# Two attention layers and two FFNs at one new token: keeping four key tiles and two value tiles on the chip between the passes

## The chip, the cores and the metric

The kernel runs on one core of a Trainium2 chip. The core has a matrix engine (PE, with its weight loads PEld), a vector engine (DVE), a scalar engine (ACT), GpSimd (POOL), and a sync engine (SP) that issues nearly all transfers; 16 DMA engines move data from HBM to SBUF. SBUF and PSUM have 128 partitions; PSUM has 8 banks of 2 KB in each partition. The metric is the device time of one launch in microseconds (us), as a median over runs.

## The reference

`B=2` rows of one token go through attention, FFN, attention, FFN, with the same weights and the same caches in both rounds:

```python
x = x + _A_ref(_layernorm(x), k_cache, v_cache, wq, wo)   # H=16, Sk=4096, Dh=256, D=448
x = x + _B_ref(_layernorm(x), W_gate, W_up, W_down)       # F=1792
x = x + _A_ref(_layernorm(x), k_cache, v_cache, wq, wo)
x = x + _B_ref(_layernorm(x), W_gate, W_up, W_down)

# _A_ref
q = (x @ wq).reshape(B, Sq, H, Dh).transpose(0, 2, 1, 3)
scores = jnp.einsum("bhqd,bhkd->bhqk", q, k_cache) * (Dh ** -0.5)
o = jnp.einsum("bhqk,bhkd->bhqd", softmax(scores), v_cache)
return o.transpose(0, 2, 1, 3).reshape(B, Sq, H * Dh) @ wo

# _B_ref
gate, up = x @ W_gate, x @ W_up
return (gate * (gate > 0) * up) @ W_down
```

All of it is float32. A head of one row has keys of 4096 x 256 and values of the same size, 4 MB each.

## The kernel before

**Units and passes.** A unit is one head of one batch row: 32 of them. Pass 1 (`first`) takes them in order 0 to 31; pass 2 (`second`) takes the last four backwards and then 0 to 27, so that what pass 1 left on the chip can be used at once. Between the passes stands the turn: the first FFN (`ffn(False)`), and after pass 2 the last FFN (`ffn(True)`). The unit that is number 12 of pass 1 (`first[12]`) is number 16 of pass 2, and `first[11]` is number 15.

**The arena.** SBUF holds one large tile, `arena`, of 27 slots of 2048 columns (1 MB each): three blocks of 8 slots, and three single slots. A block takes a pair: the values of one unit and the keys of the next one, 16384 columns or 8 MB, by one transfer (L131). Single slots take a head's projection weights (`w_head`) or a part of the FFN's weights, which are 1792 columns wide each. A transfer is issued as soon as its slots have been released (`pump`), in one fixed list for both passes, all on SP's queue. A block comes free when the keys have been reduced (`score_block`) and the values have been weighed (`weigh`). Some chunks (`keep`) stay from the end of pass 1 to the start of pass 2.

**A unit's work.** Keys lie with 32 rows of 256 in each partition; a key tile is one such row over the 128 partitions, 128 KB. In the steady part, DVE multiplies all 32 tiles by the query in place (L378, 8192 columns) and reduces them to 32 scores per partition (L386). Then come the maximum over the partitions on POOL (L429), the exponential on ACT (L434 and L437) and its sum on POOL (L443). One unit later PE multiplies the probabilities with the values (`weigh`, L462, 16 matmuls of 512 columns: two value tiles each), ACT and DVE add the two halves of the result into `row` (L475 `out_copy`, L478 `out_add`), and PE turns it into a column (L488). With every second unit PE also projects the head (L511), computes the next head's queries (L338), and ACT and POOL spread them over the partitions (L350, L354).

**Order around the change.** Each engine runs its instructions in the order in which the loop at L527 writes them: for unit `u` the scores of `u`, the end of `u-2`, the softmax of `u`, then the weighing of `u-1` and its `out_copy`.

**PSUM before.** `ps_o` has one tile `po` over two banks for the attention's output, even units in the first and odd ones in the second. `ps_f` has two rotating banks `pf` for the first queries of a pass and for the FFN's products. `ps_q`, `ps_s` and `ps_a` take the other four.

Of the kernel before, what the change touches and what calls it, by code (L numbers as in the profile page):

```python
# [27 lines left out]
ALONE = 25  # L28

# [41 lines left out]
def two_layers(  # L71
# [18 lines left out]
    ps_f = ctx.enter_context(tc.tile_pool(name="ps_f", bufs=2, space=PSUM))  # L90
# [5 lines left out]

    units = Arena()
    pending = []
    at_of = {}
    blocks = set()  # L100

    def source(key, n):
        kind, name, c = key
        if kind in "kv":
            h, b = name
            at = (h * B + b + (kind == "v")) % (H * B)
            c += NC * (kind == "k" and n < PAIR)
            return vk[at, :, c * UNIT : (c + n) * UNIT]
# [6 lines left out]
    def pump():  # L115
        while pending:
# [7 lines left out]
            dst = arena[:, at * UNIT : at * UNIT + src.shape[1]]  # L124
# [14 lines left out]

    def get(*key):  # L140
        at = at_of[key]
        return arena[:, at * UNIT : (at + 1) * UNIT]
# [90 lines left out]
    po_all = ps_o.tile([P, 2, 2 * DH], F32, name="po")  # L233
    nc.vector.memset(po_all, 0.0)
# [60 lines left out]
    def attention(order, after, q_first=None, begun=None):  # L295
# [60 lines left out]
        def first_query():  # L356


            if q_first is None:
                total = squares()  # L360
                query_of(0, ps_f.tile([P, B, DH], F32, name="pf"))
            else:
                q_of[0] = q_first
                total = begun()
            deviation(total)
            query_of(1, ps_f.tile([P, B, DH], F32, name="pf"))
# [3 lines left out]
        def score_block(u, c):  # L370
# [4 lines left out]
            if c == 0:  # L375
                s_of[u] = work.tile([P, NT], F32, name="scores")
            if c == 0:
                nc.vector.tensor_mul(kt, kt, q_of[u][:, None, :].to_broadcast([P, NT, DH]))  # L378
# [6 lines left out]
            if c == NC - 1:  # L385
                nc.vector.reduce_sum(s_of[u][:, shared:], kt[:, shared:, :], axis=AX.X)  # L386
# [65 lines left out]
        def weigh(u, c):  # L452
# [5 lines left out]
            if c == 0:  # L458
                po_of[u] = po_all[:, u % 2]
            for t in range(CT // 2):  # L460
# [4 lines left out]
                    vt[:, 2 * t * DH : (2 * t + 2) * DH],  # L465
# [94 lines left out]
    def ffn(last):  # L560
# [9 lines left out]
        def proj(parts):  # L570

            p = ps_f.tile([P, D], F32, name="pf")
# [42 lines left out]
        pg = proj([(0, 0, True), (1, 1, True), (2, 2, True), (3, 3, False)])  # L615
# [18 lines left out]
        pu = proj([(3, 4, True), (4, 0, True), (5, 1, True), (6, 2, True)])  # L634
# [8 lines left out]
        ph = ps_f.tile([P, FULL, P], F32, name="pf")  # L643
# [31 lines left out]
        if last:  # L675
# [9 lines left out]
            y_end = ps_f.tile([P, TAIL], F32, name="pf")[SUMS : SUMS + B]  # L685
            nc.tensor.matmul(y_end, unit, y_end_row, start=True, stop=False)
            pds = [po_all[:, 0, :D], ps_f.tile([P, D], F32, name="pf")] * 2
# [28 lines left out]
        q = ps_f.tile([P, DH], F32, name="pf")  # L716
# [13 lines left out]
        pd = po_all[:, 0, :D]  # L730
# [104 lines left out]
```

## Time and profile before

| | us |
|---|---|
| median of 3 runs | 1320.66 (1320.5 to 1320.78) |
| the profiled execution | 1320.27 |
| its span, first to last instruction | 1318.5 |
| DVE busy | 1081.6 |
| PE busy | 553.7 |
| POOL busy | 269.0 |
| ACT busy | 195.6 |
| moved from HBM | 562.56 MB |

The page of the profile gives, from top to bottom, busy time by engine, the span in 40 equal slices, the DMA queues, and a chain that ends with the last instruction: at each step it goes back to what released that step. A piece of the chain that is named DMA runs from the issue of a transfer to its landing, so it holds the time in which the transfer stood behind others in the queue. In groups and timelines, a bracket at the end of a row is the idle time of the engine just before the instruction, and what ended it.

### The profile page before, as it was taken

Reading aid. Unit: us, or ns where it says so; the run is one execution under the profiler, and the core shown is the slowest. Engines: PE = TensorE matmul, PEld = TensorE weight load, DVE = VectorE, ACT = ScalarE, POOL = GpSimd, SP = SyncE. Lnnn points to the kernel's source line nnn. Section 1 sums busy time; section 2 is a strip of 40 time slices with the busy share of each in tenths; the row PEclk is TensorE's granted clock in tenths of the full one; section 3 lists DMA queues with packets and bytes.
Section 4 is the critical chain, followed back from the end, with each engine's and each line's share of the span. In section 5 each row is a group of like instructions: output and inputs, shape, how many; then the busy total and the mean of one; then the engine's idle time right before and its main releaser. Section 6 shows DMA issues by size and latency. Waiting matters only on the chain.

```text
span 1318.5 us, 9085 instructions
## 1 busy us (share of the span) xinstructions
PE 553.7 (42%) x3276; PEld 190.6 (14%) x3276; DVE 1081.6 (82%) x780; ACT 195.6 (15%) x776; POOL 269.0 (20%) x192
## 2 busy tenths in 40 slices
PE   2243342433434324345585444242433424434348
PEld 2011010110111101112141111110111101101113
DVE  4989888898888988888729987798888988877892
ACT  2100000000000000212026513000000000012241
POOL 0002003322133220321001153030123331230210
PEclk9675666656667667666697777666767667666679
DMA  9999999999999999999999999999999999999998
GB/s 408 435 430 429 432 428 437 432 436 434 417 445 435 430 430 426 445 418 430 421 405 416 431 430 435 438 432 430 432 431 436 433 428 436 429 432 425 427 425 334
DMA packets 22665, 563.16 MB, mean 427 GB/s; under 512 B 2520, under 2 KB 2652, under 8 KB 9564
## 3 DMA queue, kind: packets, MB, share of 16 engines
q1 hardware_dynamic: 22612, 562.57, 99.5%
q8 instruction: 26, 0.43, 0.1%
q14 instruction: 19, 0.16, 0.0%
q10 hardware_dynamic: 8, 0.00, 0.0%
HBM read 562.56 MB, written 0.00 MB: 427 GB/s over the span
## 4 chain that ended last, share of the span: by engine, by line
DMA 55%; DVE 32%; PE 7%; POOL 2%; issue 2%; ACT 1%; DVEq 0%; SPq 0%; POOLq 0%; ACTq 0%
DMA arena<-in_vk_dram 54%; DVE arena L378 12%; DVE scores L386 11%; DVE arena L409 3%; DVE down L418 2%; PE po L462 2%; POOL top L429 2%; DVE arena L418 2%; DMA arena<-in_w_out_dram 1%; DVE row L478 1%; PE small L488 1%; PE acc L511 1%; DVE scores L415 1%; ACT arena L411 1%; PE pf L576 1%
## 5 line engine op out<-in xcount | busy, mean ns | idle before, releaser
L378 DVE TENSOR_TENSOR arena<-arena 128x8192 f32<-128x8192 f32 x51 | 443.3, 8692 | 111.0 <-DMA arena<-in_vk_dram 110.9
L386 DVE TENSOR_REDUCE scores<-arena 128x32 f32<-128x8192 f32 (+1 forms) x53 | 431.8, 8148 | 0.0
L488 PE MATMUL small<-ones,row 128*128 128x1 f32 x256 | 62.0, 346 | 686.3 <-DVE row L478 686.3
L462 PE MATMUL po<-arena,probs 128*2 128x512 f32 x2048 | 303.1, 734 | 10.3 <-DMA arena<-in_vk_dram 6.6
L429 POOL PARTITION_ALL_REDUCE top<-mx x64 | 64.6, 1009 | 645.8 <-DVE mx L427 645.8
L443 POOL PARTITION_ALL_REDUCE total<-rs x64 | 176.1, 2752 | 61.3 <-ACT probs L437 60.3
L488 PEld LDWEIGHTS small<-ones,row 128*128 128x128 f32 x256 | 56.5, 308 | 748.9 <-DVE row L478 748.9
L434 ACT ACTIVATE nm<-top,nsr 128x1 f32<-128x1 f32 x64 | 18.8, 294 | 612.4 <-POOL top L429 612.4
L354 POOL PARTITION_BROADCAST arena<-arena x58 | 27.6, 545 | 300.6 <-ACT arena L350 300.6
L462 PEld LDWEIGHTS po<-arena,probs 128*2 128x2 f32 x2048 | 54.8, 96 | 198.3 <-issue 191.2
L338 PE MATMUL pq<-arena,xs 128*33 128x256 f32 x174 | 70.6, 571 | 14.1 <-DMA arena<-in_w_head_dram 14.1
L511 PE MATMUL acc<-arena,oT 128*2 128x448 f32 x128 | 50.9, 894 | 32.1 <-DVE oT L501 32.1
L350 ACT ACTIVATE arena<-pq 33x256 f32<-33x256 f32 x29 | 10.9, 377 | 321.7 <-PE pq L342 321.7
L382 ACT ACTIVATE arena<-arena 128x256 f32<-128x256 f32 x104 | 41.7, 402 | 86.2 <-DVE arena L378 86.2
L478 DVE SCALAR_TENSOR_TENSOR row<-po,lead,row 128x256 f32<-128x256 f32 x64 | 30.7, 479 | 25.8 <-ACT row L475 25.4
L411 ACT ACTIVATE arena<-arena 128x256 f32<-128x256 f32 x117 | 47.1, 404 | 20.4 <-DVE arena L409 20.1
L409 DVE TENSOR_TENSOR arena<-arena 128x1024 f32<-128x1024 f32 (+1 forms) x24 | 42.0, 1748 | 0.0
L338 PEld LDWEIGHTS pq<-arena,xs 128*33 128x33 f32 x174 | 25.3, 162 | 81.3 <-issue 66.7
L475 ACT ACTIVATE row<-po,lead 128x256 f32<-128x256 f32 x64 | 29.1, 455 | 21.2 <-PE po L462 21.2
L418 DVE SCALAR_TENSOR_TENSOR down<-arena,pq 128x256 f32<-128x256 f32 x64 | 26.9, 420 | 5.4 <-DMA arena<-in_vk_dram 3.4
L501 DVE TENSOR_TENSOR oT<-small,ri 128x4 f32<-128x4 f32 x32 | 5.1, 161 | 29.0 <-PE small L488 29.0
L437 ACT ACTIVATE probs<-scores,nm,sr 128x32 f32<-128x32 f32 x64 | 26.4, 413 | 2.1
(145 smaller groups left out, 359.0 us busy)
## 6 DMA issues: line engine op xcount, KB each, us to landing
arena<-in_vk_dram SPq DMA_DIRECT2D x16, 4096.0 KB, 40.0
arena<-in_w_head_dram SPq DMA_DIRECT2D x31, 896.0 KB, 30.9
arena<-in_vk_dram SPq DMA_DIRECT2D x27, 1024.0 KB, 14.9
arena<-in_vk_dram SPq DMA_DIRECT2D x12, 2048.0 KB, 38.5
arena<-in_w_in_dram SPq DMA_DIRECT2D x14, 896.0 KB, 26.2
arena<-in_w_out_dram SPq DMA_DIRECT2D x5, 896.0 KB, 8.9
arena<-in_vk_dram SPq DMA_DIRECT2D x47, 43.4
arena<-in_w_out_dram SPq DMA_DIRECT2D x1, 512.0 KB, 17.3
```

What stands on the lines that cost most here:

```text
L338: nc.tensor.matmul(q, xs[:, c, :], w[:, c * DH : (c + 1) * DH], start=(c == 0), stop=False)
L378: nc.vector.tensor_mul(kt, kt, q_of[u][:, None, :].to_broadcast([P, NT, DH]))
L386: nc.vector.reduce_sum(s_of[u][:, shared:], kt[:, shared:, :], axis=AX.X)
L409: nc.vector.tensor_mul(some, some, q_of[u][:, None, :].to_broadcast([P, whole, DH]))
L411: nc.scalar.activation(kt[:, t, :], kt[:, t, :], AF.Copy, accum_out=found[:, t : t + 1])
L418: nc.vector.scalar_tensor_tensor(junk if kept else kt[:, t, :], kt[:, t, :], 1.0, q_of[u], op0=ALU.mult, op1=ALU.mult, accum_out=found[:, ...
L429: nc.gpsimd.partition_all_reduce(mx_of[u], mx, P, RED.max)
L443: nc.gpsimd.partition_all_reduce(total[:, b : b + 1], rs, P, RED.add)
L462: nc.tensor.matmul(po_of[u][32 * t : 32 * t + 2, :], p_of[u][:, n : n + 2], vt[:, 2 * t * DH : (2 * t + 2) * DH], start=(c == 0), stop=(c ...
L478: nc.vector.scalar_tensor_tensor(row[:, :DH], po_of.pop(u)[:, DH:], lead[:, 1:2], row[:, :DH], op0=ALU.mult, op1=ALU.add,)
L488: nc.tensor.matmul(pT_of[u - u % 2][:, c, b : b + 1], row[:, c * P : (c + 1) * P], ones, start=True, stop=True,)
L511: nc.tensor.matmul(acc[at : at + B], oT_of[h][:, c, :], wo[:, c * D : (c + 1) * D], start=(n < 3), stop=(n >= n_u - 3),)
```

## The change

**What stays on the chip.** In pass 1 at unit 12, ACT copies the last four key tiles of that unit (`KEYS = 4`) into two PSUM banks, `spare[0]` and `spare[1]`, two tiles of 256 columns each. At the weighing of unit 11, ACT copies its first two value tiles (`VALUES = 2`, 512 columns) into `extra`, the last 512 columns of the arena. The single slots 25 and 26 become 1792 columns wide (`place`), which is what sets those 512 columns free. In pass 2 the transfer of the pair (values of `first[11]`, keys of `first[12]`) leaves out its first 512 and its last 1024 columns: 14848 of 16384. There DVE multiplies and reduces 28 tiles in the arena and two tiles in each of the two PSUM banks, and PE takes the first two value tiles from `extra` (in pass 1 it does so as well, after the copy).

**Banks.** `ps_o` now has two tiles `po0` and `po1` of a bank each; `ps_f` has the two `spare` banks, without rotation. The first queries of pass 1 and the turn's FFN use `po0` and `po1` in place of `pf`; the last FFN uses the `spare` banks.

```diff
@@ -26,6 +26,9 @@
 WHOLE_SECOND = range(9, 29)
 KEPT = 20
 ALONE = 25
+SPARED = 12
+KEYS = 4
+VALUES = 2
 
 SUMS = 96
 HASTE = 5
@@ -87,23 +90,27 @@
     ps_o = ctx.enter_context(tc.tile_pool(name="ps_o", bufs=1, space=PSUM))
     ps_s = ctx.enter_context(tc.tile_pool(name="ps_s", bufs=2, space=PSUM))
     ps_a = ctx.enter_context(tc.tile_pool(name="ps_a", bufs=1, space=PSUM))
-    ps_f = ctx.enter_context(tc.tile_pool(name="ps_f", bufs=2, space=PSUM))
+    ps_f = ctx.enter_context(tc.tile_pool(name="ps_f", bufs=1, space=PSUM))
 
     arena = consts.tile([P, (BLOCKS * PAIR + SINGLES) * UNIT], F32, name="arena")
     ctx.enter_context(tc.manual_schedule())
 
 
 
+    extra = arena[:, -VALUES * DH :]
     units = Arena()
     pending = []
     at_of = {}
     blocks = set()
+    spared = set()
 
     def source(key, n):
         kind, name, c = key
         if kind in "kv":
             h, b = name
             at = (h * B + b + (kind == "v")) % (H * B)
+            if name in spared and n == PAIR:
+                return vk[at, :, VALUES * DH : PAIR * UNIT - KEYS * DH]
             c += NC * (kind == "k" and n < PAIR)
             return vk[at, :, c * UNIT : (c + n) * UNIT]
         if kind == "h":
@@ -121,7 +128,8 @@
                 return
             pending.pop(0)
             src = source((kind, name, c), n)
-            dst = arena[:, at * UNIT : at * UNIT + src.shape[1]]
+            start = place(at) + VALUES * DH * (name in spared and n == PAIR)
+            dst = arena[:, start : start + src.shape[1]]
             parts = [0, src.shape[1]]
             if not pending:
                 parts[1:1] = [src.shape[1] - CLOSE * TAIL]
@@ -137,9 +145,13 @@
             if n >= NC:
                 blocks.add((kind, name))
 
+    def place(at):
+        packed = max(0, at - BLOCKS * PAIR - 1)
+        return at * UNIT - packed * (UNIT - F)
+
     def get(*key):
         at = at_of[key]
-        return arena[:, at * UNIT : (at + 1) * UNIT]
+        return arena[:, place(at) : place(at + 1)]
 
     def release(*key):
         units.free.add(at_of.pop(key))
@@ -230,8 +242,10 @@
     spans += [(slice(h, h + TAIL), slice(c, c + 1)) for c, h in ((FULL, 0), (FULL + 1, TAIL))]
     rstd = consts.tile([P, B], F32, name="rstd")
 
-    po_all = ps_o.tile([P, 2, 2 * DH], F32, name="po")
-    nc.vector.memset(po_all, 0.0)
+    po = [ps_o.tile([P, 2 * DH], F32, name=f"po{i}") for i in range(2)]
+    for bank in po:
+        nc.vector.memset(bank, 0.0)
+    spare = [ps_f.tile([P, 2 * DH], F32, name=f"spare{i}") for i in range(2)]
 
 
     acc = ps_a.tile([P, D], F32, name="acc")
@@ -358,12 +372,12 @@
 
             if q_first is None:
                 total = squares()
-                query_of(0, ps_f.tile([P, B, DH], F32, name="pf"))
+                query_of(0, po[0].rearrange("p (b n) -> p b n", b=B))
             else:
                 q_of[0] = q_first
                 total = begun()
             deviation(total)
-            query_of(1, ps_f.tile([P, B, DH], F32, name="pf"))
+            query_of(1, po[1].rearrange("p (b n) -> p b n", b=B))
             unread = work.tile([P, 1], F32, name="sums")
             nc.scalar.activation(unread, eps_t, AF.Exp)
 
@@ -374,8 +388,24 @@
             kt = arena[:, at : at + NC * UNIT].rearrange("p (t n) -> p t n", t=NT)
             if c == 0:
                 s_of[u] = work.tile([P, NT], F32, name="scores")
+            there = [(kt, 0)]
+            if order[u] == first[SPARED]:
+                most = NT - KEYS
+                held = [bank.rearrange("p (t n) -> p t n", t=2) for bank in spare]
+                there = [(kt[:, :most], 0)]
+                there += [(part, most + 2 * i) for i, part in enumerate(held)]
+                if not ahead:
+                    if c == 0:
+                        for part, t in there[1:]:
+                            nc.scalar.activation(part, kt[:, t : t + 2, :], AF.Copy)
+                        spared.add(order[u])
+                    there[1:] = [(kt[:, most:], most)]
             if c == 0:
-                nc.vector.tensor_mul(kt, kt, q_of[u][:, None, :].to_broadcast([P, NT, DH]))
+                for part, t in there:
+                    n = part.shape[1]
+                    nc.vector.tensor_mul(
+                        part, part, q_of[u][:, None, :].to_broadcast([P, n, DH])
+                    )
             shared = 0 if (WHOLE_SECOND if ahead else WHOLE_FIRST)[0] <= u < ALONE else CT
             if c == 0:
                 for t in range(shared):
@@ -383,7 +413,11 @@
                         kt[:, t, :], kt[:, t, :], AF.Copy, accum_out=s_of[u][:, t : t + 1]
                     )
             if c == NC - 1:
-                nc.vector.reduce_sum(s_of[u][:, shared:], kt[:, shared:, :], axis=AX.X)
+                if shared or not ahead:
+                    there = [(kt[:, shared:, :], shared)]
+                for part, t in there:
+                    found = s_of[u][:, t : t + part.shape[1]]
+                    nc.vector.reduce_sum(found, part, axis=AX.X)
                 blocks.remove(("k", order[u]))
                 for k in range(NC):
                     release("k", order[u], k)
@@ -456,13 +490,16 @@
             if (u - n_u, c) in FILL:
                 busy(FILL[u - n_u, c])
             if c == 0:
-                po_of[u] = po_all[:, u % 2]
+                po_of[u] = po[u % 2]
+            held = c == 0 and order[u] == first[SPARED - 1]
+            if held and not ahead:
+                nc.scalar.activation(extra, vt[:, : VALUES * DH], AF.Copy)
             for t in range(CT // 2):
                 n = c * CT + 2 * t
                 nc.tensor.matmul(
                     po_of[u][32 * t : 32 * t + 2, :],
                     p_of[u][:, n : n + 2],
-                    vt[:, 2 * t * DH : (2 * t + 2) * DH],
+                    extra if held and t == 0 else vt[:, 2 * t * DH : (2 * t + 2) * DH],
                     start=(c == 0),
                     stop=(c == NC - 1),
                 )
@@ -567,9 +604,11 @@
             h, b = second[0]
             w_q = get("h", h, 0)
 
-        def proj(parts):
-
-            p = ps_f.tile([P, D], F32, name="pf")
+        banks = spare if last else po
+
+        def proj(p, parts):
+
+            p = p[:, :D]
             for n, (part, c, done) in enumerate(parts):
                 w = get("in", "", part)
                 for j in range(4):
@@ -612,7 +651,7 @@
 
 
 
-        pg = proj([(0, 0, True), (1, 1, True), (2, 2, True), (3, 3, False)])
+        pg = proj(banks[0], [(0, 0, True), (1, 1, True), (2, 2, True), (3, 3, False)])
         add_rows(SUMS, lead, stop=last)
         if last:
             y_left = y[:, : FULL * P]
@@ -631,7 +670,7 @@
         nc.scalar.activation(hid, pg, AF.Relu)
         if not last:
             cols = ps_q.tile([P, DH], F32, name="pq")
-        pu = proj([(3, 4, True), (4, 0, True), (5, 1, True), (6, 2, True)])
+        pu = proj(banks[1], [(3, 4, True), (4, 0, True), (5, 1, True), (6, 2, True)])
         if not last:
             turn_cols = w_q[:, FULL * DH + P + 2 * D :]
             nc.scalar.activation(turn_cols, cols, AF.Copy, scale=nscaled[:, b : b + 1])
@@ -640,7 +679,7 @@
             unit = ident[SUMS : SUMS + B, SUMS : SUMS + B]
             nc.tensor.matmul(y_left, unit, left, start=True, stop=False)
 
-        ph = ps_f.tile([P, FULL, P], F32, name="pf")
+        ph = banks[0][:, : FULL * P].rearrange("p (m r) -> p m r", m=FULL)
         ph_tail = ps_q.tile([P, P], F32, name="pq")
         for m in range(FULL):
             nc.tensor.transpose(ph[:, m, :], hid[:, m * P : (m + 1) * P], ident)
@@ -682,9 +721,9 @@
                 nc.vector.tensor_mul(
                     close[:, i, :], square, st.rearrange("p (b r) -> p b r", b=B)[:, :, 0]
                 )
-            y_end = ps_f.tile([P, TAIL], F32, name="pf")[SUMS : SUMS + B]
+            y_end = spare[1][SUMS : SUMS + B, :TAIL]
             nc.tensor.matmul(y_end, unit, y_end_row, start=True, stop=False)
-            pds = [po_all[:, 0, :D], ps_f.tile([P, D], F32, name="pf")] * 2
+            pds = [po[0][:, :D], spare[0][:, :D]] * 2
 
             def to_y(at, stop):
                 nc.tensor.matmul(y[:, at], scaled, down[:, at], start=False, stop=stop)
@@ -713,7 +752,7 @@
 
 
 
-        q = ps_f.tile([P, DH], F32, name="pf")
+        q = po[0][:, :DH]
 
         def ask(c):
             x_c = xT[:, c, b : b + 1].to_broadcast([P, P])
@@ -727,7 +766,7 @@
                     start=False, stop=(c == FULL + 1),
                 )
 
-        pd = po_all[:, 0, :D]
+        pd = po[1][:, :D]
         sums = work.tile([P, FULL + 1], F32, name="sums4")
         total = work.tile([P, 1], F32, name="sums")
         for c in range(FULL + 1):
```

The built programs show three places. The first is ACT around unit 12 of pass 1 (`probs` is written by the exponential, `row<-po` is `out_copy`; numbers are buffers). Before, the exponential of unit 11, `out_copy` of unit 10, the two steps of unit 12's softmax, `out_copy` of unit 11, and a query's copy:

```order
L437 ACTIVATE probs_632,rs_633<-scores_606,nm_630,sr_135 128x32
L475 ACTIVATE row_79<-po_108,lead_94 128x256
L434 ACTIVATE nm_667<-top_665,nsr_134 128x1
L437 ACTIVATE probs_669,rs_670<-scores_654,nm_667,sr_135 128x32
L475 ACTIVATE row_79<-po_108,lead_94 128x256
L350 ACTIVATE arena_76<-pq_702 33x256
```

Now, at the same place:

```order
L471 ACTIVATE probs_634,rs_635<-scores_608,nm_632,sr_139 128x32
L512 ACTIVATE row_79<-po0_108,lead_94 128x256
L400 ACTIVATE spare0_112<-arena_76 128x512
L400 ACTIVATE spare1_113<-arena_76 128x512
L468 ACTIVATE nm_672<-top_670,nsr_138 128x1
L471 ACTIVATE probs_674,rs_675<-scores_656,nm_672,sr_139 128x32
L496 ACTIVATE arena_76<-arena_76 128x512
L512 ACTIVATE row_79<-po1_109,lead_94 128x256
L364 ACTIVATE arena_76<-pq_708 33x256
```

The two copies to PSUM stand ahead of unit 12's softmax; the copy of unit 11's value tiles stands behind it and ahead of `out_copy` of unit 11.

The second is DVE at unit 16 of pass 2, from the multiply to the maximum. Before:

```order
L378 TENSOR_TENSOR arena<-arena 128x8192
L478 SCALAR_TENSOR_TENSOR row<-po,lead,row 128x256
L450 RECIPROCAL ri<-total 128x2
L386 TENSOR_REDUCE scores<-arena 128x32
L427 TENSOR_REDUCE mx<-scores 128x1
```

Now:

```order
L406 TENSOR_TENSOR arena<-arena 128x7168
L406 TENSOR_TENSOR spare_112<-spare_112,arena 128x512
L406 TENSOR_TENSOR spare_113<-spare_113,arena 128x512
L515 SCALAR_TENSOR_TENSOR row<-po_108,lead,row 128x256
L484 RECIPROCAL ri<-total 128x2
L420 TENSOR_REDUCE scores<-arena 128x28
L420 TENSOR_REDUCE scores<-spare_112 128x2
L420 TENSOR_REDUCE scores<-spare_113 128x2
L461 TENSOR_REDUCE mx<-scores 128x1
```

One multiply and one reduction have become three each, over the same number of columns.

The third is SP in pass 2, from the pairs of units 14 and 15 on. Before:

```order
L131 DMA arena<-in_w_head_dram 128x1792
L131 DMA arena<-in_vk_dram 128x16384 x2
L131 DMA arena<-in_w_head_dram 128x1792
L131 DMA arena<-in_vk_dram 128x16384 x2
L131 DMA arena<-in_w_head_dram 128x1792
```

Now:

```order
L139 DMA arena<-in_w_head_dram 128x1792
L139 DMA arena<-in_vk_dram 128x16384 x2
L139 DMA arena<-in_w_head_dram 128x1792
L139 DMA arena<-in_vk_dram 128x14848
L139 DMA arena<-in_vk_dram 128x16384
L139 DMA arena<-in_w_head_dram 128x1792
```

One transfer is shorter; the number of transfers and their order are the same.

## The prediction

> **What bounds the kernel now.** I read the page first: busy times, DMA slices, queues, chain.
>
> ```profile
> PE 553.7 (42%) x3276; PEld 190.6 (14%) x3276; DVE 1081.6 (82%) x780; ACT 195.6 (15%) x776; POOL 269.0 (20%) x192
> DMA  9999999999999999999999999999999999999998
> GB/s 408 435 430 429 432 428 437 432 436 434 417 445 435 430 430 426 445 418 430 421 405 416 431 430 435 438 432 430 432 431 436 433 428 436 429 432 425 427 425 334
> q1 hardware_dynamic: 22612, 562.57, 99.5%
> DMA 55%; DVE 32%; PE 7%; POOL 2%; issue 2%; ACT 1%; DVEq 0%; SPq 0%; POOLq 0%; ACTq 0%
> ```
>
> No engine is as full as the transfers: 99.5% of the span of 16 DMA engines is packets, and no slice but the last shows a gap. The chain gives DVE 32%, but that is no sign of a vector bound. The chain through three units, in order of time (start, duration, what), shows why:
>
> ```profile
> 932.14 43.37 DMA arena<-in_vk_dram
> 975.64 8.69 DVE arena L378
> 984.33 0.40 DVE row L478
> 984.80 8.59 DVE scores L386
> 993.45 42.31 DMA arena<-in_vk_dram
> 1035.79 8.69 DVE arena L378
> ```
>
> A DMA piece starts with a reduction's end and lasts 42 to 43 us, about two units, because two other pairs stand ahead in the queue. So the chain goes back through a release that came early, while the engines that move the data never paused. Two stretches of pass 2, each from the start of one multiply to that of another (18 units, and six of them from unit 16), confirm it. Columns: start and end, us, busy time of PE, PEld, DVE, ACT and POOL, clock, DMA share, GB/s:
>
> ```profile
> 851.94:1220.97 369.03, 137.41 (x774) 44.49 (x774) 317.20 (x90) 34.39 (x129) 81.07 (x54) 0.67 1.00 431
> 975.64:1098.30 122.66, 45.30 (x258) 14.73 (x258) 107.87 (x30) 8.09 (x27) 32.67 (x18) 0.67 1.00 433
> ```
>
> DMA share 1.00, DVE 107.87 of 122.66 us: a unit takes 122.66 / 6 = 20.4 us of transfers and 18.0 us of DVE. **The time is the bytes over the rate**, plus a start and a tail.
>
> **The change part by part.** The sum is made against the profiled execution (1320.27 us, span 1318.5); the median is 0.39 us above it.
>
> *Bytes removed.* 512 + 1024 columns x 128 partitions x 4 bytes = 786,432 bytes, once, in pass 2. At the 433 GB/s of the stretch that holds this transfer: 0.786 MB / 433 GB/s = **1.82 us**. Bounds: the fastest slice on the page, 445 GB/s, gives 1.77 us; the slowest 10 us of the turn, 391 GB/s (below), 2.01 us. I take 1.82, since that row is of long rows like those shortened. All later transfers stand behind this one in one queue, so each lands 1.82 us earlier, if nothing else stops the queue.
>
> The Trainium skill, HBM Reference, section Specifications, puts a core's effective share of HBM at about 358 GB/s; by that figure the saving would be an estimated 2.20 us. The stretches above show 431 and 433, so this trace disagrees for a core that runs alone, as the same section allows.
>
> *Unit 12 of pass 1.* The work there, with unit 11's weighing (PE) and the next multiply; and where the pair released there (for unit 15) is issued and used:
>
> ```profile
> 262.60 8.69 DVE L378 TENSOR_TENSOR arena<-arena 128x8192 f32<-128x8192 f32 x1 [2.48 <-DMA arena<-in_vk_dram]
> 272.68 6.52 PE L462 MATMUL po<-arena,probs 128*2 128x512 f32 x32
> 280.41 0.33 SPq L131 DMA_DIRECT2D arena<-in_vk_dram  x1
> 281.36 0.41 ACT L437 ACTIVATE probs<-scores,nm,sr 128x32 f32<-128x32 f32 x1
> 281.77 0.45 ACT L475 ACTIVATE row<-po,lead 128x256 f32<-128x256 f32 x1
> 281.91 8.69 DVE L378 TENSOR_TENSOR arena<-arena 128x8192 f32<-128x8192 f32 x1 [1.36 <-DMA arena<-in_vk_dram]
> 290.52 0.48 DVE L478 SCALAR_TENSOR_TENSOR row<-po,lead,row 128x256 f32<-128x256 f32 x1
> 322.82 8.69 DVE L378 TENSOR_TENSOR arena<-arena 128x8192 f32<-128x8192 f32 x1 [1.31 <-DMA arena<-in_vk_dram]
> ```
>
> For durations, the groups with their forms apart (count, busy us, mean ns):
>
> ```profile
> L378 DVE TENSOR_TENSOR arena<-arena 128x8192 f32<-128x8192 f32 x51 | 443.3, 8692 | 111.0 <-DMA arena<-in_vk_dram 110.9
> L386 DVE TENSOR_REDUCE scores<-arena 128x32 f32<-128x8192 f32 x40 | 346.8, 8671 | 0.0
> L409 DVE TENSOR_TENSOR arena<-arena 128x1024 f32<-128x1024 f32 x12 | 14.6, 1216 | 0.0
> L415 DVE TENSOR_REDUCE scores<-arena 128x4 f32<-128x1024 f32 x8 | 9.8, 1220 | 0.3
> L638 DVE TENSOR_TENSOR row<-pf,row 128x448 f32<-128x448 f32 x2 | 1.2, 624 | 7.9 <-PE pf L576 7.9
> L631 ACT ACTIVATE row<-pf 128x448 f32<-128x448 f32 x2 | 1.1, 536 | 0.0
> ```
>
> A copy of 448 columns on ACT takes 0.54 us; 512 at the same rate 0.61. The two copies to PSUM start when the keys land, at 262.6, and end by about 263.9. The multiply of the last four tiles stands behind a multiply of 28: from 8692 ns at 8192 columns and 1216 at 1024, a column costs 1.043 ns and an instruction 0.15 us, so 28 tiles take 7.62 us, to 270.2. The copies have 6 us to spare; if they had none, DVE would wait 1.2 us, inside the 1.36 us it idles before the next multiply. The split itself adds 0.15 us to DVE.
>
> The copy of the value tiles is another matter: on ACT it stands behind unit 12's exponential, so the weighing that ran from 272.68 now starts after 281.77 + 0.61 = 282.4, lasts 6.52 us at the same slow clock, and ends at 288.9. Behind it on ACT is `out_copy` (0.45 us, to 289.4); behind that DVE's `out_add`, which stands after the next multiply and is not due before 290.52. Behind it on SP is the pair for unit 15, whose slots hold those values: issued at 280.41 before, about 288.9 now, **8.5 us later**. It was needed by unit 15's multiply at 322.82; its own 8.39 MB take 19.4 us at 433 GB/s, so its turn in the queue came at 303.4. A load on an empty queue, the first of the kernel, gives the lead it needs:
>
> ```profile
> arena<-in_w_head_dram SPq DMA_DIRECT2D x1, 896.0 KB, 4.7
> arena<-in_w_out_dram SPq DMA_DIRECT2D x1, 896.0 KB, 7.8
> ```
>
> 4.7 us to landing, of which 0.917 MB / 433 GB/s = 2.1 is the moving: 2.6 us of lead. Due by 300.8, issued at 288.9: 11.9 us left. Cost nothing; without that cover it would be one for one. (The second row is used below.)
>
> *Unit 16 of pass 2.* 28 tiles in the arena, 4 in PSUM. L638 reads PSUM: 448 columns in 0.624 us, so 512 cost 0.69; the reduction's slope from 8671 and 1220 gives 7.61 for 28 tiles and 0.69 for two. Sum: 7.62 + 0.69 x 2 + 7.61 + 0.69 x 2 = 17.99 us, against 8.69 + 8.67 = 17.36: 0.63 more. No row shows a multiply written to PSUM or a reduction from it; from no penalty to double time on these four, the bound is 0.6 to 3.4 us. DVE's idle time before units 16 and 17:
>
> ```profile
> 975.64 8.69 DVE L378 TENSOR_TENSOR arena<-arena 128x8192 f32<-128x8192 f32 x1 [2.45 <-DMA arena<-in_vk_dram]
> 994.93 8.69 DVE L378 TENSOR_TENSOR arena<-arena 128x8192 f32<-128x8192 f32 x1 [1.33 <-DMA arena<-in_vk_dram]
> ```
>
> The shorter transfer eats 1.82 of the 2.45, the longer work 0.63 of the 1.33. Even at 3.4 us DVE would be late for a unit or two only, and releases have the cover of some 20 us computed above. Nothing.
>
> *The turn and the start.* Shapes and order of the FFN's instructions stay; only banks differ, and every earlier reader of `po0` and `po1` stands ahead of the FFN on a path PE already waits for. The start clears two banks in two instructions, long before any slot is released. Nothing.
>
> Sum: 1320.27 - 1.82 = 1318.45 for a run like the profiled one, **1318.84** for the median.
>
> **The rivals.** *More than the bytes.* The turn moves less than the steady part:
>
> ```profile
> 660.00:670.00 10.00, 9.41 (x68) 3.44 (x64) 2.29 (x12) 2.39 (x4) 0.00 (x0) 1.00 0.96 397
> 670.00:680.00 10.00, 9.18 (x73) 3.58 (x65) 1.42 (x6) 1.17 (x3) 0.00 (x0) 1.00 0.97 391
> 680.00:690.00 10.00, 8.79 (x142) 6.07 (x138) 2.90 (x16) 3.05 (x16) 0.00 (x0) 1.00 1.02 421
> 690.00:700.00 10.00, 5.79 (x22) 4.11 (x22) 9.86 (x48) 7.08 (x30) 0.99 (x3) 0.83 1.02 415
> ```
>
> Against 433 GB/s these 40 us lack 40 - 10 x (397 + 391 + 421 + 415) / 433 = 2.5 us. If part of it is the queue running thin, for which 7.8 us to landing speaks, and the new banks shorten the FFN, a third could return: 1318.84 - 0.9 = 1317.9. Against: shares of 0.96 to 1.02 mean busy engines, so the loss is of the short rows moved there, and the banks remove no wait.
>
> *Hidden.* Something else than transfers sets the end, and the saving is lost: 1320.7. For it: the last FFN's chain of PE and DVE. Against: its last products wait for the weights, not the reverse:
>
> ```profile
> 1314.98 0.47 PE L669 MATMUL pf<-arena,row 128*32 128x64 f32 x18 [0.17 <-DMA arena<-in_w_out_dram]
> ```
>
> *Slower: the late pair.* Place: the copy of value tiles on ACT, the weighing of unit 11 behind it, and SP's pair for unit 15. It decides when the issue comes 20.4 us late (300.8 - 280.41) instead of 8.5; from there the queue runs dry one for one. If the weighing slipped by another unit, 20.4 us, the issue would come at 309.3, 8.5 too late: 1318.84 + 8.5 = 1327.3. Against: nothing on ACT between the exponential and the copy waits for anything.
>
> **How the numbers follow.** Forecast 0.75, more than the bytes 0.13, hidden 0.07, slower 0.05. A run-to-run spread of 0.3 us and the 0.39 between profile and median put the forecast's own range at 1318.3 to 1319.3; out to the first rival and some way to the second it is 1317.9 to 1319.8, which leaves out the slow case and nearly all of the hidden one. About 0.2% (2.64 us, so 1318.02 and 1323.30) is what a measurement of this kernel can tell from no change. The forecast, at -1.82, lies within it but for 0.02 of its chance: faster 0.13 + 0.02 = 0.15, same 0.73 + 0.07 = 0.80, slower 0.05.
>
> **What would show it.** In the changed profile: HBM bytes 562.56 less 0.79; DMA share still 1.00; unit 15's pair of pass 1 issued near 289 and its multiply still within 0.3 us of 322.8; the multiplies of pass 2 after unit 16 all about 1.8 us earlier, DVE's idle time before unit 16 near 0.6; a last product that waits for weights. The prediction is wrong if a stretch shows a DMA share under 1.00 near 300 or 1000, or if the late units come 1.8 us earlier and the end does not.

## The result, and the profile after

| | before | after |
|---|---|---|
| median, us (22 runs each) | 1320.76 | 1318.89 |
| lowest to highest, us | 1320.32 to 1321.43 | 1318.63 to 1319.81 |
| profiled execution, its span, us | 1320.27, 1318.5 | 1318.79, 1316.9 |

The ratio of after to before is 0.9986, with a 95% interval of 0.998 to 0.9992. The gain is 1.87 us; the forecast was 1318.84 us, a gain of 1.82. As a share it is 0.14%, so by the bound of 0.2% that the prediction set it is "about the same", though the interval leaves out 1.

The page of the changed kernel: the busy times, the DMA share and GB/s of 40 slices, the main queue, the shares of the chain.

```profile
PE 567.2 (43%) x3276; PEld 191.9 (15%) x3276; DVE 1082.2 (82%) x786; ACT 197.4 (15%) x779; POOL 283.5 (22%) x192
DMA  9999999999999999999999999999999999999998
GB/s 406 438 430 426 437 428 431 440 436 426 422 446 430 428 433 424 441 426 431 420 399 419 431 430 440 426 438 428 434 433 436 430 430 432 428 436 426 426 425 332
q1 hardware_dynamic: 22612, 561.79, 99.5%
DMA 57%; DVE 29%; PE 8%; POOL 2%; issue 2%; ACT 1%; DVEq 0%; SPq 0%; POOLq 0%; ACTq 0%
```

The queue moved 0.78 MB less in as many packets and was again full for 99.5% of the span. DVE has six instructions more, ACT three more; POOL's 14.5 us more are in its all-reduces, of which the last experiments tell more. The same two stretches of pass 2 as before, multiply to multiply:

```profile
852.15:1219.38 367.23, 144.66 (x774) 45.94 (x774) 317.46 (x95) 34.39 (x129) 87.44 (x54) 0.65 1.00 432
974.02:1096.70 122.68, 48.95 (x258) 15.63 (x258) 108.13 (x35) 9.18 (x31) 39.41 (x19) 0.67 1.00 432
```

The 18 units take 367.23 us where they took 369.03: 1.80 us less. The six units from unit 16 on take what they took (122.68 and 122.66), so the step lies in the stretch that ends with unit 16's start. The timeline of DVE shows it at unit 16 of pass 2 (start, duration, and in brackets the idle time before):

```profile
974.02 7.63 DVE L406 TENSOR_TENSOR arena<-arena 128x7168 f32<-128x7168 f32 x1 [0.62 <-POOL top L463]
981.57 1.29 DVE L406 TENSOR_TENSOR spare<-spare,arena 128x512 f32<-128x512 f32 x2
983.23 7.60 DVE L420 TENSOR_REDUCE scores<-arena 128x28 f32<-128x7168 f32 x1
990.74 1.28 DVE L420 TENSOR_REDUCE scores<-spare 128x2 f32<-128x512 f32 x2
993.31 8.69 DVE L406 TENSOR_TENSOR arena<-arena 128x8192 f32<-128x8192 f32 x1 [1.06 <-DMA arena<-in_vk_dram]
```

Both multiplies over the arena, at 974.02 and 993.31, start 1.62 us earlier than before. This execution had run 0.2 us behind the one of before until then (852.15 against 851.94), so the step is 1.82 to 1.83 us. The bracket at 974.02 names POOL's all-reduce, which had ended 0.1 us before, and not the transfer; a landing 1.82 us earlier than before would fall at the same moment (975.64 + 0.21 - 1.82 = 974.03), and this row does not tell the two apart. The wait at 993.31 is for the transfer. The step is still there at the multiply of 1219.38 (1220.97 before, so 1.59 earlier) and in the span, 1.6 us shorter.

In pass 1 the release of unit 11's values came late, as forecast. SP, ACT, PE and DVE around unit 12, and the multiply that uses the pair issued there:

```profile
262.74 1.12 ACT L400 ACTIVATE spare<-arena 128x512 f32<-128x512 f32 x2 [0.62 <-DMA arena<-in_vk_dram]
281.68 0.41 ACT L471 ACTIVATE probs<-scores,nm,sr 128x32 f32<-128x32 f32 x1
282.09 0.61 ACT L496 ACTIVATE arena<-arena 128x512 f32<-128x512 f32 x1
282.76 6.42 PE L499 MATMUL po<-arena,probs 128*2 128x512 f32 x32 [9.69 <-ACT arena L496]
289.30 0.33 SPq L139 DMA_DIRECT2D arena<-in_vk_dram  x1
303.80 8.69 DVE L406 TENSOR_TENSOR arena<-arena 128x8192 f32<-128x8192 f32 x1 [2.88 <-DMA arena<-in_vk_dram]
323.07 8.69 DVE L406 TENSOR_TENSOR arena<-arena 128x8192 f32<-128x8192 f32 x1 [1.31 <-DMA arena<-in_vk_dram]
```

PE now waits 9.69 us for the copy, and the pair for unit 15 is issued at 289.30 instead of 280.41. Its multiply starts at 323.07 against 322.82, with 1.31 us of idle time ahead of it as before: the 0.25 us is this execution's offset. The last product still waits for its weights, not they for it:

```profile
1313.43 0.47 PE L708 MATMUL spare<-arena,row 128*32 128x64 f32 x18 [0.16 <-DMA arena<-in_w_out_dram]
```

### The profile page after: what moved, and what is told of

Read it like the earlier page. It is cut to its first block, busy times and chain, and to the rows that moved or that the text cites. A ratio compares the mean times of both kernels' runs of the same rounds, so it can differ in the third digit from the quotient of the medians.

```text
span 1316.9 us, 9091 instructions
## 1 busy us (share of the span) xinstructions
PE 567.2 (43%) x3276; PEld 191.9 (15%) x3276; DVE 1082.2 (82%) x786; ACT 197.4 (15%) x779; POOL 283.5 (22%) x192
## 3 DMA queue, kind: packets, MB, share of 16 engines
q1 hardware_dynamic: 22612, 561.79, 99.5%
## 4 chain that ended last, share of the span: by engine, by line
DMA 57%; DVE 29%; PE 8%; POOL 2%; issue 2%; ACT 1%; DVEq 0%; SPq 0%; POOLq 0%; ACTq 0%
DMA arena<-in_vk_dram 56%; DVE arena L406 12%; DVE scores L420 10%; PE po L499 3%; DVE arena L443 3%; POOL top L463 2%; DVE arena L452 2%; DMA arena<-in_w_out_dram 1%; PE acc L548 1%; PE pq L352 1%; DVE row L515 1%; PE small L525 1%; DVE down L452 1%; DVE scores L449 1%; ACT arena L445 1%
## 5 line engine op out<-in xcount | busy, mean ns | idle before, releaser
L406 DVE TENSOR_TENSOR arena<-arena 128x8192 f32<-128x8192 f32 (+2 forms) x52 | 442.3, 8508 | 108.5 <-DMA arena<-in_vk_dram 107.8
L420 DVE TENSOR_REDUCE scores<-arena 128x32 f32<-128x8192 f32 (+2 forms) x53 | 430.8, 8128 | 0.0
L499 PE MATMUL po<-arena,probs 128*2 128x512 f32 x2048 | 315.0, 759 | 20.0 <-ACT arena L496 9.7
L477 POOL PARTITION_ALL_REDUCE total<-rs x64 | 190.7, 2980 | 61.3 <-ACT probs L471 60.3
L445 ACT ACTIVATE arena<-arena 128x256 f32<-128x256 f32 x117 | 47.1, 404 | 20.4 <-DVE arena L443 20.1
```

Of the source, the lines that this page charges most:

```text
L406: nc.vector.tensor_mul(part, part, q_of[u][:, None, :].to_broadcast([P, n, DH]))
L420: nc.vector.reduce_sum(found, part, axis=AX.X)
L445: nc.scalar.activation(kt[:, t, :], kt[:, t, :], AF.Copy, accum_out=found[:, t : t + 1])
L477: nc.gpsimd.partition_all_reduce(total[:, b : b + 1], rs, P, RED.add)
L499: nc.tensor.matmul(po_of[u][32 * t : 32 * t + 2, :], p_of[u][:, n : n + 2], extra if held and t == 0 else vt[:, 2 * t * DH : (2 * t + 2) * ...
```

## The experiments

Theory: the gain is the bytes over the rate of a full queue, and the rest of the change has cover. Its rivals: the new banks or the shorter turn do part of it; the bytes alone would be lost; the late pair costs something. Afterwards two runs measure the cover itself, one takes the gain further, and four ask how far it can be taken.

### The banks alone

The changed kernel with nothing kept; the new banks and slots stay:

```diff
-            if order[u] == first[SPARED]:
+            if False:
...
-            held = c == 0 and order[u] == first[SPARED - 1]
+            held = False
```

> The changed kernel without the six kept tiles: nothing is copied aside and the pair is loaded whole; the new banks of the FFN and of the first queries stay. If the time is bytes over the rate, this is the kernel before: 1320.7 us, ratio 1.000, and the stretch from 660 to 700 us moves what it moved before. If the new banks shorten the turn and that is worth time (more than the bytes), it comes out at about 1319.8, ratio 0.9993 or lower, and unit 9's multiply in pass 2 comes about 0.9 us earlier.

Measured: 1320.69 us against 1320.62, ratio 1.0001 (0.9992 to 1.001). The interval alone would still allow the rival's 0.9993; the trace does not. Unit 9's multiply in pass 2 starts at 830.74 us against 830.35 in the kernel before, so it is not earlier, and the four stretches of the turn moved 394, 382, 423 and 417 GB/s, no faster than the 397, 391, 421 and 415 of before. The same stretches in the full change:

```profile
660.00:670.00 10.00, 8.95 (x63) 3.27 (x59) 2.29 (x12) 2.39 (x4) 0.00 (x0) 1.00 0.96 394
670.00:680.00 10.00, 9.18 (x73) 3.46 (x64) 1.28 (x5) 1.17 (x3) 0.00 (x0) 1.00 0.95 372
680.00:690.00 10.00, 9.05 (x143) 6.26 (x142) 2.78 (x14) 2.81 (x14) 0.00 (x0) 1.00 1.02 423
690.00:700.00 10.00, 4.12 (x22) 2.90 (x22) 9.86 (x48) 7.32 (x31) 0.95 (x2) 1.00 1.01 418
```

The rival "more than the bytes" falls.

### The bytes alone

The kernel before with the one pair shortened by the same 1536 columns and nothing kept in their place:

```diff
+            if name in cut and n == PAIR:
+                return vk[at, :, 512 : PAIR * UNIT - 1024]
...
-    attention(second, set(), *ffn(False))
+    begun = ffn(False)
+    cut.update([first[12]])
+    attention(second, set(), *begun)
```

> The kernel before with one edit: the pair for unit 16 of pass 2 leaves out the same 1536 columns, and nothing is kept in their place, so that unit computes with what its block held earlier. No copies, no pieces in PSUM, no new banks. If the time is bytes over the rate, it gains the whole 1.82 us: 1318.9 us, ratio 0.9986, equal to the changed kernel. If the saved bytes are hidden and the change's gain came from elsewhere, it stays at 1320.7.

Measured: 1318.93 us, ratio 0.9987 (0.9979 to 0.9996): the whole gain of the change. So neither copies nor the longer unit 16 cost anything that shows, and "hidden" falls as well.

### The late pair, undone

The copy of the value tiles is moved ahead of unit 12's softmax, behind the copies to PSUM:

```diff
                             nc.scalar.activation(part, kt[:, t : t + 2, :], AF.Copy)
+                        vt = get("v", order[u - 1], 0)
+                        nc.scalar.activation(extra, vt[:, : VALUES * DH], AF.Copy)
...
-            if held and not ahead:
-                nc.scalar.activation(extra, vt[:, : VALUES * DH], AF.Copy)
```

> The changed kernel with the copy of the two value tiles moved on ACT from behind unit 12's exponential to behind the two copies into PSUM, before that softmax. Then unit 11's weighing should start near 273 us instead of 282.8 and the pair for unit 15 be issued near 280.7 instead of 289.3, some 8.6 us earlier. If the late pair is wholly covered by the pairs ahead of it in the queue, the time does not move: 1318.9 us. If lateness cost anything, it would fall by up to the part that was not covered; by the sum of the prediction that part is 0.

Measured: 1318.81 us, ratio 0.9987 (0.9978 to 0.9996). SP's issue and the multiply of unit 15:

```profile
280.97 0.33 SPq L139 DMA_DIRECT2D arena<-in_vk_dram  x1
323.20 8.69 DVE L408 TENSOR_TENSOR arena<-arena 128x8192 f32<-128x8192 f32 x1 [1.33 <-DMA arena<-in_vk_dram]
```

The issue is 8.3 us earlier than in the changed kernel, the multiply no earlier. The lateness was covered in full.

### How much cover there is

The changed kernel, but the slots of unit 11's values are held until a dummy copy on ACT behind unit 13's exponential, of 2 columns:

```diff
-            if ("v", order[u], c) not in after:
+            if not ahead and order[u] == first[SPARED - 1]:
+                late.append((u, c))
+            elif ("v", order[u], c) not in after:
...
+            if late:
+                for v, c in late[:1]:
+                    some = get("v", order[v], c)[:, :2]
+                    nc.scalar.activation(some, some, AF.Copy)
+                for v, c in late:
+                    release("v", order[v], c)
+                late.clear()
```

> The changed kernel with the slots of unit 11's values held back: a copy of two columns of them onto themselves on ACT, behind unit 13's exponential, must end before the pair for unit 15 is issued, so it goes out near 302.6 us instead of 289.3. By the prediction's sum it is due by 300.8: the queue should run dry for about 1.8 us, and the time be 1318.9 + 1.8 = 1320.7. If the cover is larger than worked out, 1318.9; if the pairs ahead cover nothing, 1318.9 + 13.3 = 1332.

The second kernel copies four times 2048 columns there (`late[:4]`, `[:, :2048]`).

> As the run before it, with four copies of 2048 columns (about 1.9 us each) in place of the small one: the pair for unit 15 goes out near 310.0 us, 9.2 us after it is due. If the cover ends at 300.8 and lateness beyond it counts one for one: 1318.9 + 9.2 = 1328.1 us, and 7.4 us more than the run before it. If the loss is made up later (releases come early again, the queue fills up), it would be less; idle transfer time cannot be made up if transfers set the end.

Measured: 1319.73 us, ratio 0.9994 (0.9984 to 1.0003), and 1327.28 us, ratio 1.005 (1.0035 to 1.0064). The first time is 1.0 us under its expectation of 1320.7, the second 0.8 us under 1328.1. The profiled execution of the first took 1321.89 us (the other nine 1319.51 to 1320.19), that of the second 1328.25, so their rows show somewhat more loss than the medians. The first kernel, with SP's issue, 5 us of the windows (the last two columns are DMA share and GB/s), and the multiplies of units 14 and 15:

```profile
302.10 0.33 SPq L139 DMA_DIRECT2D arena<-in_vk_dram  x1
300.00:305.00 5.00, 0.00 (x0) 0.00 (x0) 2.10 (x3) 1.25 (x5) 0.74 (x2) 0.70 0.78 275
303.45 8.69 DVE L406 TENSOR_TENSOR arena<-arena 128x8192 f32<-128x8192 f32 x1 [2.87 <-DMA arena<-in_vk_dram]
324.98 8.69 DVE L406 TENSOR_TENSOR arena<-arena 128x8192 f32<-128x8192 f32 x1 [3.56 <-DMA arena<-in_vk_dram]
```

The second kernel, the same rows:

```profile
310.68 0.33 SPq L139 DMA_DIRECT2D arena<-in_vk_dram  x1
300.00:305.00 5.00, 2.26 (x24) 0.32 (x16) 2.52 (x3) 2.34 (x4) 0.74 (x2) 1.00 0.18 79
305.00:310.00 5.00, 0.00 (x0) 0.00 (x0) 5.00 (x1) 5.00 (x4) 0.00 (x0) 0.57 0.00 0
310.00:315.00 5.00, 1.34 (x8) 1.04 (x12) 5.00 (x4) 1.02 (x2) 0.00 (x0) 0.50 0.87 315
304.51 8.69 DVE L406 TENSOR_TENSOR arena<-arena 128x8192 f32<-128x8192 f32 x1 [2.45 <-DMA arena<-in_vk_dram]
333.87 8.69 DVE L406 TENSOR_TENSOR arena<-arena 128x8192 f32<-128x8192 f32 x1 [11.39 <-DMA arena<-in_vk_dram]
```

The queue runs dry: in the second kernel nothing moves from 305 to 310 us, where ACT copies. From issue to multiply it is 22.88 and 23.19 us; 19.4 of them are the moving, so a transfer on a dry or nearly dry queue takes 3.5 to 3.8 us on top of its moving. Not all of that lies ahead of the first byte: the second kernel's row of 310 to 315 us shows 315 GB/s, 1.6 MB, where a start 3.8 us behind the issue at 310.68 would leave time for 0.2. How the rest divides was not taken apart.

From unit 14's multiply to unit 15's it is 21.53 and 29.36 us against 19.27 in the changed kernel: the queue lost 2.3 and 10.1 us. The second issue is 8.58 us later, or 7.5 less the 1.06 by which that execution's unit 14 was later; the queue lost 7.8 us more, and the medians differ by 7.55: one for one. Against the changed kernel the medians lost 0.84 and 8.4 us, so 1.5 and 1.7 us of what the queue lost in the profiled executions do not show in them (the spans of those executions are 3.1 and 9.5 us longer). The second kernel's multiplies trail those of the changed kernel by 10.8 us at unit 15 (0.7 of it from before), 11.0 at 527 us, 10.2 at 569, 9.8 at 765 and 9.5 from 830 on. No cause was found for this, and that the first 2.3 us count in full is not shown.

### Two more key tiles

From the changed kernel: a third PSUM bank for two more key tiles, taken from the pool of small tiles, and the early copy of the values:

```diff
-KEYS = 4
+KEYS = 6
...
-    ps_s = ctx.enter_context(tc.tile_pool(name="ps_s", bufs=2, space=PSUM))
+    ps_s = ctx.enter_context(tc.tile_pool(name="ps_s", bufs=1, space=PSUM))
...
-    spare = [ps_f.tile([P, 2 * DH], F32, name=f"spare{i}") for i in range(2)]
+    spare = [ps_f.tile([P, 2 * DH], F32, name=f"spare{i}") for i in range(KEYS // 2)]
...
-        minus = ps_s.tile([P, B], F32, name="small")
+        minus = ps_q.tile([P, B], F32, name="pq")
```

> The changed kernel with six key tiles kept instead of four: a third PSUM bank for them is taken from the small rotating tiles, which get one bank instead of two (one small product at the turn moves to the bank of the queries), and the value copy stands early. 262,144 bytes fewer than the changed kernel: at 433 GB/s 0.61 us. If the time is bytes over the rate and the small tiles' second bank was needed by nothing on the path: 1318.3 us, ratio to the kernel before 0.9982. If the single bank of small tiles makes PE and DVE wait on the path at the end, the gain is eaten by some tenths of a microsecond: 1318.5 to 1319.0.

Measured: 1318.2 us against 1320.62, ratio 0.9981 (0.9973 to 0.999). That is 2.42 us off, and 512 columns more at 433 GB/s make 1.82 + 0.61 = 2.43. It is the fastest kernel here that computes the reference; its interval overlaps that of the changed kernel, so the 0.6 us between them rests on the bytes and on the medians. One row of unit 16 of pass 2 foretells what limits this saving:

```profile
973.70 7.17 POOL L465 PARTITION_ALL_REDUCE top<-mx  x1 [2.82 <-DVE mx L463]
```

The keys have now landed by the time DVE has its maximum, so the multiply (26 tiles in the arena, 7.09 us from 973.56) starts ahead of POOL's all-reduce of that maximum, which takes 7.17 us in place of 0.35. In this one unit it cost nothing that shows; the next experiments show what it does in twenty.

### How far it goes: all 20 whole pairs shortened

The second experiment's kernel with every whole pair of pass 2 shortened by 1536 columns, and then by 4608:

```diff
-    cut.update([first[12]])
+    cut.update(second[u] for u in WHOLE_SECOND)
```

> The kernel before with all 20 whole pairs of pass 2 shortened by the same 1536 columns, nothing kept in their place (those units compute with what the blocks held earlier). 20 x 0.786 MB = 15.73 MB, at 433 GB/s 36.3 us. If every byte saved is time saved: 1284.4 us, ratio 0.9725. A unit then needs 18.6 us of transfers (8.06 MB with half a head's weights), and DVE's own round is 18.0 us for even units and 19.2 for odd ones (from the starts of multiplies and ends of maxima at 262.6 to 300.9 us), 18.6 on average, so the two meet here: if waits between units add up, the gain ends at 34 to 36 us. If the saved bytes were hidden behind other work, the time would stay above 1310.

> As the run before it, with three times the columns left out of each of the 20 pairs (4608 of 16384). Bytes alone would give 109 us: 1211.8. But transfers then take only 15.0 us a unit and DVE's round is 18.6 us, so if a unit's time is the longer of the two, the gain stops at 20 x (20.4 - 18.6) = 37 us plus what the end saves: about 1284 us, hardly below the run before it, with a DMA share well under 1.00 (about 0.8) from 850 to 1200 us.

Measured: 1302.23 us (ratio 0.9856, 0.984 to 0.9873) and 1298.77 us (0.9833, 0.9819 to 0.9848). Half of the gain is missing in the first, and three times the bytes bring only 3.5 us more. Both were expected at about 1284 us, with a DVE round of 18.6 us. The windows of the first, with the DMA share and GB/s last, show the end without transfers (its span is 1300.7 us):

```profile
851.94:1160.00 308.06, 119.32 (x644) 38.10 (x646) 276.63 (x79) 22.14 (x78) 149.10 (x45) 0.65 0.99 426
1280.00:1310.00 30.00, 17.82 (x227) 8.93 (x226) 5.47 (x25) 4.11 (x11) 0.00 (x0) 1.00 0.07 28
```

The transfers ended early and something else set the end. POOL is at 149 us of 308, where it was at 81 of 369 in the kernel before. Two units of its steady part in the windows, and one in the timeline:

```profile
947.38:987.46 40.08, 14.62 (x86) 4.73 (x86) 35.97 (x11) 2.70 (x9) 19.09 (x6) 0.70 1.00 430
...
968.02 8.69 DVE L382 TENSOR_TENSOR arena<-arena 128x8192 f32<-128x8192 f32 x1
968.27 8.65 POOL L433 PARTITION_ALL_REDUCE top<-mx  x1 [3.40 <-DVE mx L431]
977.70 0.45 ACT L479 ACTIVATE row<-po,lead 128x256 f32<-128x256 f32 x1
978.18 0.48 DVE L482 SCALAR_TENSOR_TENSOR row<-po,lead,row 128x256 f32<-128x256 f32 x1 [1.47 <-ACT row L479]
987.46 8.68 DVE L382 TENSOR_TENSOR arena<-arena 128x8192 f32<-128x8192 f32 x1
```

Two units take 40.08 us, 20.04 each, with 35.97 us of DVE in them, though its multiply no longer waits for a transfer. The all-reduce of the maximum, started 0.25 us into the multiply, ends with it. So the exponential and `out_copy` come late, and `out_add` on DVE waits 1.47 us in every unit: 35.97 of work, twice 1.47, and a wait of 1.10 for PE in the other of the two units, which the kernel before has too, make 40.0. The kernel with three times the columns left out has the same round, 40.08 us for two units (964.66 to 1004.74), at a DMA share of 0.81. In the kernel before the same all-reduce falls into the time in which DVE waits for keys, and takes 0.35 us; the one of the sum, which in every second unit starts inside the multiply there, takes 8.87:

```profile
993.69 0.35 POOL L429 PARTITION_ALL_REDUCE top<-mx  x1 [18.64 <-DVE mx L427]
995.00 8.87 POOL L443 PARTITION_ALL_REDUCE total<-rs  x1 [0.96 <-ACT probs L437]
```

### The multiply in two instructions

If POOL is held by the one instruction beside which it starts, a short first piece lets it go. The first kernel of the last pair (1536 columns), with each whole multiply of pass 2 as 4 and 28 tiles, and as 16 and 16:

```diff
-                nc.vector.tensor_mul(kt, kt, q_of[u][:, None, :].to_broadcast([P, NT, DH]))
+                cuts = [0, 4, NT] if ahead else [0, NT]
+                for lo, hi in zip(cuts, cuts[1:]):
+                    nc.vector.tensor_mul(
+                        kt[:, lo:hi],
+                        kt[:, lo:hi],
+                        q_of[u][:, None, :].to_broadcast([P, hi - lo, DH]),
+                    )
```

> The kernel e3_all (the kernel before with all 20 whole pairs of pass 2 shortened by 1536 columns; what they leave out is computed from stale contents) with one edit: each whole multiply of pass 2 is two instructions, the first of 4 tiles (1.2 us), the second of 28 (7.6 us). e3_all took 1302.23 us where its bytes alone would give 1284.3, and in its trace POOL's all-reduce of the maximum, started 0.2 us into DVE's multiply, ends with it after 8.65 to 8.72 us, so that ACT's out_copy comes late and DVE's out_add waits 1.47 us in each unit: a DVE round of 20.04 us. Theory A (POOL is held while the one DVE instruction runs that it started beside): the all-reduce ends behind the small multiply, after 1.0 to 1.7 us; out_add no longer waits; the round falls to (40.08 - 2 x 1.47 + 2 x 0.15) / 2 = 18.7 us, as long as the shortened transfers, and the time to 1284 to 1289. Theory B (POOL is held as long as DVE has such work, or the all-reduce is simply slow in this place): 8.7 us still, time 1302 to 1306.

> e3_all with each whole multiply of pass 2 as two instructions of 16 tiles (4.4 us each). Leaves out what e3_all leaves out. Theory A (POOL is held by one instruction): the all-reduce takes about 4.2 us, half of 8.65; everything behind it is done before the second half ends, so out_add does not wait either: time 1284 to 1289, as with a small first piece. Theory B: 8.7 us, 1302 to 1306. A third reading, that the all-reduce is slowed in a fixed ratio rather than held to an end, would give the same figure of POOL in both kernels.

Measured: 1284.42 us (ratio 0.973, 0.9713 to 0.9746) and 1284.58 us (0.9729, 0.9714 to 0.9743). With 4 and 28 tiles (the row of x2 holds both pieces of the multiply):

```profile
978.96 8.75 DVE L384 TENSOR_TENSOR arena<-arena 128x1024 f32<-128x1024 f32 x2
979.13 1.25 POOL L439 PARTITION_ALL_REDUCE top<-mx  x1 [9.12 <-DVE mx L437]
981.35 6.60 POOL L453 PARTITION_ALL_REDUCE total<-rs  x1 [0.96 <-ACT probs L447]
987.62 0.48 DVE L488 SCALAR_TENSOR_TENSOR row<-po,lead,row 128x256 f32<-128x256 f32 x1
```

With 16 and 16:

```profile
980.20 8.75 DVE L384 TENSOR_TENSOR arena<-arena 128x4096 f32<-128x4096 f32 x2
980.37 4.45 POOL L439 PARTITION_ALL_REDUCE top<-mx  x1 [13.45 <-DVE mx L437]
988.86 0.48 DVE L488 SCALAR_TENSOR_TENSOR row<-po,lead,row 128x256 f32<-128x256 f32 x1
```

The all-reduce takes as long as the piece it starts beside, 1.25 and 4.45 us instead of 8.65; `out_add` has no idle time before it; and the time falls to the bytes: 20 x 0.786 MB at 433 GB/s are 36.3 us, 1320.63 - 36.3 = 1284.3. Each ends about 0.2 us behind its piece. So POOL is held to the end of one DVE instruction. A slowing in a fixed ratio, which would give the same figure in both kernels, is ruled out, and with 4 and 28 tiles the second all-reduce takes 6.60 us, to the end of the piece of 28. The Trainium skill, "SBUF — State Buffer", section "SBUF: two separate sides", says that a DVE operation with two inputs in SBUF and a GpSimd operation that reads SBUF exclude each other over the whole of whichever starts first. These rows agree with it: 1.25, 4.45 and 8.65 us beside pieces of 4, 16 and 32 tiles.

## Why the prediction was right, point by point

- **The bound.** Right: a full queue before and after (99.5%, share 1.00). From 280 to 330 us, around the late pair, the share is 1.02 at 441 GB/s. The bytes alone gave 1318.93 us, the change 1318.89. That the forecast of 1318.84 is only 0.05 us off is luck: the median before moved by 0.1 us between 3 runs and 22.
- **Bytes removed, 1.82 us.** Right in size: the step at unit 16 is 1.82 to 1.83 us. Measured on twenty times the bytes, with the multiply split: 15.73 MB in 36.2 us, 434 GB/s. By the Trainium skill's figure of 358 GB/s ("HBM Reference", "Specifications"), which the prediction set beside it, the estimate would have been 43.9 us. One reading was off without harm: the stretch with 433 GB/s starts when this transfer has landed; the one that holds it shows 431, which gives 1.82 too.
- **Unit 12 of pass 1.** Right: copies 1.12 us together, from 262.74; value copy at 282.09 (forecast 281.77), weighing from 282.76, the pair's issue at 289.30 (forecast 288.9), no cost. That cover hides it was shown both ways, by undoing the lateness (no gain) and by raising it beyond the cover (7.5 us more lateness, 7.55 us more time).
- **The lead of 2.6 us, mis-sized.** It came from a first transfer on an empty queue, up to its landing; a pair on a dry one took 3.5 to 3.8 beyond its moving, up to its multiply. So the pair was due near 300, not 300.8, and the cover left was nearer 11 us than 11.9. The point of decision for the slower rival moves by about a microsecond; its form (dry from there, one for one) held from the first late kernel to the second, while the first lost only 0.84 us.
- **Unit 16 of pass 2, +0.63 us.** Forecast with no penalty for PSUM, and there is none: two multiplies 1.29 us, two reductions 1.28. The unit got only 0.27 us longer: 974.02 to 992.25 (993.31 less the idle 1.06) is 18.23 us, against 975.64 to 993.60, 17.96. The rows of neighbouring instructions overlap by some 0.1 us, which a sum of durations does not see. Idle time before unit 16 was 0.62, near the forecast 0.6, though its bracket names POOL.
- **18.0 us of DVE in a unit of 20.4, wrong as a measure of room.** The prediction set the one against the other, as if 2.4 us were free. Busy time is not the round: once DVE no longer waits for keys, POOL's all-reduce falls into the multiply and the round is 20.04 us, which leaves 0.4. It did not matter for one shortened transfer. For twenty it halved the gain that the expectation forecast.
- **The turn and the start, nothing.** Right, by the run with the banks alone.
- **The rivals.** "More than the bytes" and "hidden" each fell to one run. (In the first, a third of 2.5 us is 0.8, not 0.9; both lie inside the range.) "Slower" exists as a mechanism, from some 10 to 11 us of lateness beyond what the change brought, and it was not reached.

## What to carry to other kernels

In a kernel whose one queue is full from start to end, a byte saved is worth its share of that queue's rate, and everything else is a question of cover: take the time of the late issue, the time at which its turn comes, and the lead of a dry queue. How far such savings go is not read from an engine's busy time, since an engine that waits for transfers may be hiding stalls in that wait. Take away the wait, in a kernel that leaves the bytes out, and look at the round that remains.

## What was not expected of the hardware

- A GpSimd all-reduce over 128 partitions took 0.35 us alone and 8.65 us when it started inside DVE's 8.69 us multiply. Cutting the multiply in two, which costs DVE under 0.1 us a unit (8.75 against 8.69), was worth 17.8 us (1302.23 to 1284.42) where DVE set the pace.
- DVE's work on keys in PSUM ran at the speed of SBUF: 692 ns for a multiply in place and 680 ns for a reduction of 512 columns, where the rows of SBUF give 0.68 and 0.69 us by their slope.
- A transfer issued to a dry or nearly dry queue was in use 3.5 to 3.8 us later than its bytes take at 433 GB/s, against 2.6 us to landing worked out for the kernel's first load.
